# One more attention layout for batches 1 to 7: shared query rows, wider transposes, one transpose burst

## The chip, the cores and the metric

The kernel runs on one core of one Trainium2 chip. The metric is the device time of one execution in microseconds (us); lower is better. The engines are named as in the profile: PE (TensorE matmul), PEld (its weight loads), DVE (VectorE), ACT (ScalarE), POOL (GpSimd) and SP (SyncE, which here only issues DMAs).

## What is computed

Eight batches of attention with eight heads, 576 positions and 64 columns per head, are followed by a MoE layer without routing. The attention has two parts that are added. One is local: each position attends to the positions less than 4 away. The other is coarse: q, k and v are averaged over groups of 4 positions, 144 rows attend to 144 rows, and each result row is repeated 4 times. Cut to its core:

```python
out_d = sm_attn(mean4(q), mean4(k), mean4(v))      # 144 x 144 per head
out_up = np.repeat(out_d, 4, axis=2)
scores = np.where(abs(i - j) < 4, scale * q @ k.T, -1e9)
out_local = softmax(scores) @ v
x = (out_up + out_local).transpose(0, 2, 1, 3).reshape(B * S, H * D)   # 4608 x 512
h = x @ w_in                                       # 512 x 2048
return (h / (1 + exp(-1.702 * h))) @ w_out         # 2048 x 512
```

## The kernel before

**Groups and steps.** The MoE runs over nine groups of 512 tokens. A group has 64 matmuls of 512 columns for the first layer (`mm1`, line 717 in `hps_mm`) and 64 for the second (`mm2`, line 781). While group g runs, the attention of batch g + 1 is put between these matmuls in steps written out by hand: `attention` (line 666) returns a list of functions, and `POS` (line 810) says ahead of which step of the group each is issued. Steps below 16 count blocks of four matmuls of `mm1`; from 16 on, step n stands ahead of matmul n - 16 of `mm2`. Group 0 has its own list, `POS_0` (line 811). Batch 0 is computed ahead of all groups by functions of its own (names ending in 0).

Every engine executes its instructions in program order. What a step issues on ACT or DVE therefore stands ahead of what later matmuls need from these engines.

**One batch.** Two head pairs share a score step. `scores_mixed` (line 401) writes local and coarse scores into three double banks of PSUM (`PA`, three tiles of two banks each), ACT exponentiates them (lines 415 and 421), and DVE multiplies the local ones by the mask (line 429). Then four head pairs `hp` follow, each through these stages:

- `av` (line 431): 20 local and 20 coarse matmuls of 65 columns (64 of v and one that gives the sum for the normalisation), in 64x64 tiles of the array. The local rows come in five chunks with two key halves (`par`), for two heads `j`. Rows of head 0 and head 1 lie on different halves of the partitions (`pos = j if par == 0 else 1 - j`).
- `normalise` (line 476): a reciprocal and a multiplication on DVE, from PSUM into y in bf16.
- `transp` (line 491): 20 matmuls with the identity for the local part and 6 for the coarse part, in 64x64 tiles, into an fp32 double bank x.
- `copy_od` (line 620): ACT copies the coarse part out of x, each column four times, into od in fp32; od has two buffers.
- `merge` (line 637): DVE adds x and od into `xT`, which `mm1` of the next group reads. One addition takes 570 columns and a second one the 6 columns at both ends.

In batches 2 to 7 the steps are: scores 0, exponentials 0, scores and exponentials 1, `av` and `normalise` of pairs 0 and 1 (step 45), `av` of pairs 2 and 3 with `transp` of pair 0 (step 56), `transp` and `merge` of pairs 1 to 3 (step 69). Batch 1 has nine steps: `av` of pairs 0 and 1 (46), `transp` of 0 (52), of 1 (56), `av` of 2 and 3 (65), `transp` of 2 (71), of 3 (75).

**Output and loads.** When 16 matmuls of `mm2` have filled a bank, ACT evicts it into osb (line 766) and SP stores it. Two single banks (`PM`) take turns there; `mm1` uses the same two, and for its second tile one bank of PA. In group 0, `mm2` holds four output tiles at once, two of them in PA[0]. The loads of q and k are issued by POOL, those of v by SP; `load_v4` follows the last step of the batch.

Of the kernel before, what the change touches and what calls it, by code (L numbers as in the profile page):

```python
# [8 lines left out]
FP32 = mybir.dt.float32  # L9
BF16 = mybir.dt.bfloat16  # L10
AF = mybir.ActivationFunctionType
ALU = mybir.AluOpType
# [7 lines left out]
def kernel(  # L20
# [409 lines left out]

    def av(b, hp, n=None):
        o = ps_tile(n)
        av_local(b, hp, o)
        av_down(b, hp, o)
        return o

    def banks(t):
        return t if t is PM else [t[:, u, :] for u in range(2)]

    def av_local(b, hp, o, chunks=range(5)):  # L440
        E, vb, o = es[hp], vbs[b % 2], banks(o)
        for i in chunks:
            for par in range(2):
                for j in range(2):
                    pos = j if par == 0 else 1 - j
                    nc.tensor.matmul(  # L446
                        o[par][64 * pos : 64 * pos + 64, 65 * i : 65 * i + 65],
                        lhsT=E[64 * par : 64 * par + 64, j, 60 * i : 60 * i + 64],
                        rhs=vb[64 * par : 64 * par + 64, i, 2 * hp + j, :],
                        start=True, stop=True,  # L450
                        tile_position=(64 * par, 64 * pos),
                    )

    def av_down(b, hp, o):
        Ed, vd, u, o = eds[hp // 2], vds[b % 2], hp % 2, banks(o)

        blocks = [(kc, x, 0) for kc in range(3) for x in range(2)]
        blocks += [(0, 0, 1), (0, 1, 1), (1, 0, 1), (2, 0, 1)]
        if True:
            for kc, x, c2 in blocks:  # L460
                for j in range(2):
                    pos = j if x == 0 else 1 - j
                    c0 = 65 * (5 + c2)
                    q0 = SD * kc + 48 * (min(x + c2, 1) + x)
                    last = x == c2 == 1
                    if last:
                        q0 = 0
                    nc.tensor.matmul(  # L468
                        o[j][64 * pos : 64 * pos + 64, c0 : c0 + 65],
                        lhsT=Ed[64 * j : 64 * j + 48, u, q0 : q0 + 64],  # L470
                        rhs=vd[64 * j : 64 * j + 48, kc, hp, :],
                        start=(kc == 0), stop=(kc == 2 or last),
                        tile_position=(64 * j, 64 * pos),
                    )

    def normalise(o):
        y = work.tile([128, 2, 7, D], BF16, name="y", tag="y", bufs=4)
        rc = work.tile([128, 2, 7, 1], FP32, name="rc", tag="rc")
        for xs in (slice(0, 1), slice(1, 2)) if o is PM else (slice(0, 2),):
            n = xs.stop - xs.start  # L480
            ov = (o[xs.start][:, None, :] if o is PM else o)[:, :, 0:455].rearrange(
                "p x (c e) -> p x c e", e=65
            )
            nc.vector.reciprocal(rc[:, xs], ov[:, :, :, 64:65])
            nc.vector.tensor_tensor(  # L485
                out=y[:, xs], in0=ov[:, :, :, 0:D],
                in1=rc[:, xs].to_broadcast([128, n, 7, D]), op=ALU.mult,
            )
        return y

    def transp(y, n=None):
        x = ps_tile(n)
        for i in range(5):
            for par in range(2):
                for j in range(2):
                    pos = j if par == 0 else 1 - j
                    c0 = 0 if (par == 1 or i == 0) else 3
                    c1 = 60 if (par == 0 or i == 4) else 57
                    nc.tensor.matmul(  # L499
                        x[64 * j : 64 * j + 64, par, 57 * i + c0 : 57 * i + c1],  # L500
                        lhsT=y[64 * pos : 64 * pos + 60, par, i, :],
                        rhs=ident(pos, 60, c0, c1),
                        start=True, stop=True,
                        tile_position=(64 * pos, 64 * j),
                    )
        for c2, xx in ((0, 0), (0, 1), (1, 0)):
            for j in range(2):
                pos = j if xx == 0 else 1 - j
                nc.tensor.matmul(  # L509
                    x[64 * j : 64 * j + 64, xx, 288 + 48 * c2 : 336 + 48 * c2],  # L510
                    lhsT=y[64 * pos : 64 * pos + 48, j, 5 + c2, :],
                    rhs=ident(pos, 48, 0, 48),
                    start=True, stop=True,
                    tile_position=(64 * pos, 64 * j),
                )
        return x

    def av_local0(hp, o, chunks):
        E, vb = es[hp], vbs[0]
# [98 lines left out]
            )  # L618

    def copy_od(x):  # L620
        od = work.tile([128, S], FP32, name="od", tag="od")
        for xx, t0, n in ((0, 0, 96), (1, 96, 48)):
            nc.scalar.copy(  # L623
                out=od[:, 4 * t0 : 4 * (t0 + n)].rearrange("p (t f) -> p t f", f=4),
                in_=x[:, xx, 288 : 288 + n, None].to_broadcast([128, n, 4]),
            )
        return od

# [5 lines left out]

    def merge(b, hp, x, od, eng=None):
        t0 = b * S
        eng = eng or nc.vector
        if eng is nc.gpsimd:  # L640
            xs = work.tile([128, 2, 512], BF16, name="xs", tag="xs", bufs=2)
            nc.scalar.copy(out=xs[:, :, 0:288], in_=x[:, :, 0:288])
            x = xs
        eng.tensor_tensor(  # L644
            out=sub(xT[hp], t0 + 3, (57, 2), (114, 5), (1, 57)),
            in0=sub(x, 3, (509, 2), (57, 5), (1, 57)),
            in1=sub(od, 3, (57, 2), (114, 5), (1, 57)),
            op=ALU.add,
        )
        eng.tensor_tensor(  # L650
            out=sub(xT[hp], t0, (573, 2), (1, 3)),
            in0=sub(x, 0, (512 + 285, 2), (1, 3)),
            in1=sub(od, 0, (573, 2), (1, 3)),
            op=ALU.add,
        )

    def warm(n, cols=512, t=None, z=wz):
        t = pm_tile() if t is None else t  # L660
# [5 lines left out]
    def attention(b, slots=None):  # L666
# [23 lines left out]
                    st["y", hp] = normalise(st["o", hp])  # L690
            return f

        def tr(*hps):
            def f():
                for hp in hps:
                    st["x", hp] = transp(st["y", hp], slots and slots[hp % 2])
                for hp in hps:
                    od = copy_od(st["x", hp])
                    merge(b, hp, st["x", hp], od)
            return f  # L700
# [5 lines left out]
        def av_tr():  # L706
            for hp in (2, 3):
                st["o", hp] = av(b, hp)
            st["x", 0] = transp(st["y", 0])
            for hp in (2, 3):  # L710
                st["y", hp] = normalise(st["o", hp])
            merge(b, 0, st["x", 0], copy_od(st["x", 0]))

        return first + [av_tr, tr(1, 2, 3)]

    def hps_mm(g, ffc, dmc, acc):
        nc.tensor.matmul(  # L717
# [261 lines left out]
```

## Time and profile before

| what | value |
|---|---|
| median of 3 runs | 320.72 us (318.91 to 321.6) |
| profiled execution, own time | 320.13 us |
| its span, first to last instruction | 318.4 us |
| mean granted TensorE clock | 0.995 |
| instructions | 10941 |
| DMA packets | 64078, 40.02 MB |

The span is what the profile shows; the execution's own time is 1.7 us longer, for what lies around it. A line of the profile names the source line, the engine, the operation, what is written and read (out<-in), the count, the busy time or the mean duration, and the idle time before it with what ended it. "issue" as the releaser means that the engine waited for nothing that the profile shows. Durations of matmuls include their latency, so that many overlap; starts say more than durations. Some matmul records are missing from the trace; the weight loads are all there.

### The profile page before, as it was taken

How to read it: one execution, taken by the hardware profiler on the slowest of the kernel's cores; microseconds unless marked ns; L12 is line 12 of the kernel's file. 1: busy time of each engine (PE TensorE's matmuls, PEld its weight loads, DVE VectorE, ACT ScalarE, POOL GpSimd, SP SyncE). 2: the span in 40 equal slices, each digit the busy share in tenths (PEclk: the TensorE clock that was granted, in tenths of full speed). 3: DMA queues.
4: the chain of work that ended last, by engine and by line, in shares of the span. 5: the costliest groups of instructions: out<-in, count | busy, mean ns of one | idle time of the engine just before them, and what ended most of it. 6: DMA issues, size and time to landing. Idle time of an engine off the chain costs nothing.

```text
span 318.4 us, 10941 instructions
## 1 busy us (share of the span) xinstructions
PE 301.9 (95%) x4872; PEld 156.5 (49%) x4923; DVE 130.3 (41%) x219; ACT 184.9 (58%) x320; POOL 138.7 (44%) x170
## 2 busy tenths in 40 slices
PE   7699999999899999999999999999999999999995
PEld 4465454545454555445545454445445544444444
DVE  5855625831575047704780288017811650000000
ACT  5445782567546684659465846584667556415611
POOL 8773790099227940695059604980294000000000
PEclk9979999999999999999999999999999999999999
DMA  7999999999949923995299619961810210020011
GB/s 120 118 200 209 182 126 213 166 229 227 165 128 203 207 64 103 190 209 101 72 197 205 128 48 213 206 136 39 176 41 3 70 68 2 0 99 33 2 65 67
DMA packets 64078, 40.02 MB, mean 126 GB/s; under 512 B 44064, under 2 KB 55456, under 8 KB 64032
## 3 DMA queue, kind: packets, MB, share of 16 engines
q1 hardware_dynamic: 44496, 24.32, 37.3%
q0 software_dynamic: 19392, 14.95, 33.8%
q8 instruction: 38, 0.62, 0.9%
q14 instruction: 8, 0.07, 0.1%
q10 hardware_dynamic: 144, 0.07, 0.1%
HBM read 44.83 MB, written 9.44 MB: 170 GB/s over the span
## 4 chain that ended last, share of the span: by engine, by line
PE 91%; issue 3%; DMA 2%; DVE 1%; POOL 1%; ACT 1%; POOLq 0%
PE pm L781 35%; PE pm L717 35%; PE pa L717 4%; PE pa L365 2%; PE pa L377 2%; DMA qb<-in_q_dram 2%; PE pa L781 2%; PE pa L446 2%; PE pa L499 2%; PE pa L468 2%; PE pm L796 1%; PE pm L334 1%; PE pa L509 0%; PE pa L524 0%; DVE qT L267 0%
## 5 line engine op out<-in xcount | busy, mean ns | idle before, releaser
L717 PE MATMUL pm<-xT,w_in_bf 128*128 128x512 bf16 x495 | 118.2, 379 | 1.2 <-ACT xT L616 0.2
L781 PE MATMUL pm<-w_out_bf,gT 128*128 128x512 bf16 x499 | 114.4, 379 | 4.2 <-issue 4.1
L728 ACT ACTIVATE gT<-pm 128x512 bf16<-128x512 f32 x128 | 76.3, 598 | 43.7 <-PE pm L717 43.7
L717 PEld LDWEIGHTS <-w_in_bf 128*128 128x128 bf16 x576 | 55.7, 98 | 66.5 <-issue 0.5
L781 PEld LDWEIGHTS <-gT 128*128 128x128 bf16 x560 | 52.1, 98 | 60.1 <-issue 0.8
L429 DVE TENSOR_TENSOR es<-es,mask 128x600 bf16<-128x600 bf16 x28 | 17.6, 643 | 94.6 <-ACT es L415 93.8
L297 POOL TENSOR_TENSOR pq<-kT 128x576 f32<-128x576 bf16 x13 | 15.1, 1165 | 70.5 <-DVE kT L267 70.5
L766 ACT ACTIVATE osb<-pm 128x512 f32<-128x512 f32 (+2 forms) x35 | 20.5, 586 | 38.2 <-PE pm L781 30.3
L623 ACT COPY od<-pa 128x384 f32<-128x384 f32 (+1 forms) x56 | 19.0, 407 | 27.2 <-PE pa L509 20.7
L485 DVE TENSOR_TENSOR y<-pa,rc 128x896 bf16<-128x896 f32 x28 | 30.6, 1092 | 1.0
L415 ACT ACTIVATE es<-pa 128x600 bf16<-128x600 f32 x32 | 19.7, 668 | 9.5 <-PE pa L365 9.4
L644 DVE TENSOR_TENSOR xT<-pa,od 128x570 bf16<-128x570 f32 x28 | 21.0, 752 | 8.8 <-ACT od L623 8.8
L313 POOL TENSOR_TENSOR v<-v 112x512 f32<-112x512 f32 x18 | 23.0, 1279 | 0.0
L768 DVE TENSOR_SCALAR osb<-pm 128x128 f32<-128x128 f32 x1 | 0.3, 291 | 55.0 <-ACT osb L766 55.0
L267 DVE STREAM_TRANSPOSE kT<-kb 128x576 f32<-128x576 f32 x16 | 20.0, 1250 | 4.3 <-DMA kb<-in_k_dram 4.2
L267 DVE STREAM_TRANSPOSE qT<-qb 128x576 f32<-128x576 f32 x16 | 19.9, 1242 | 0.6 <-POOL kdT L301 0.2
L717 PE MATMUL pa<-xT,w_in_bf 128*128 128x512 bf16 x64 | 20.0, 379 | 0.0
L307 POOL CAST vb<-vf 128x2560 bf16<-128x2560 f32 x6 | 13.9, 2319 | 13.7 <-DMA vf<-in_v_dram 11.3
L365 PEld LDWEIGHTS <-kT 32*64 32x64 bf16 x1280 | 14.2, 104 | 7.7 <-issue 4.9
L365 PE MATMUL pa<-qT,kT 32*64 32x60 bf16 x1280 | 16.4, 198 | 1.3 <-DVE qT L267 1.3
L221 POOL DMA_DIRECT2D vb<-in_v_dram x20 | 13.7, 698 | 9.1 <-DMA w_in_bf<-in_moe_w_in_dram 4.0
L297 POOL TENSOR_TENSOR pq<-qT 128x576 f32<-128x576 bf16 x14 | 16.0, 1145 | 0.1
(90 smaller groups left out, 274.2 us busy)
## 6 DMA issues: line engine op xcount, KB each, us to landing
out_dram<-osb SPq DMA_DIRECT2D x35, 256.0 KB, 2.1
vf<-in_v_dram SPq DMA_DIRECT2D x60, 128.0 KB, 6.8
v<-in_v_dram SPq DMA_DIRECT2D x36, 192.0 KB, 5.5
kb<-in_k_dram POOLq DMA_DIRECT2D x16, 288.0 KB, 7.2
qb<-in_q_dram POOLq DMA_DIRECT2D x16, 288.0 KB, 8.6
w_in_bf<-in_moe_w_in_dram POOLq DMA_DIRECT2D x4, 512.0 KB, 7.2
w_out_bf<-in_moe_w_out_dram POOLq DMA_DIRECT2D x4, 512.0 KB, 12.9
vb<-in_v_dram POOLq DMA_DIRECT2D x20, 64.0 KB, 6.4
```

Of the source, the lines that this page charges most:

```text
L267: nc.vector.transpose(out=t32.rearrange("p (i c) -> p c i", c=18), in_=store[b, qd].bitcast(FP32).rearrange("p (c d) -> p c d", c=18),)
L297: nc.gpsimd.tensor_tensor(out=t1, in0=sv[:, :, 0:2, :], in1=sv[:, :, 2:4, :], op=ALU.add)
L313: eng.tensor_tensor(out=t1[0:112], in0=x[:, :, 0:2, :], in1=x[:, :, 2:4, :], op=ALU.add)
L365: nc.tensor.matmul(sp[r // 2][64 * par : 64 * par + 64, r % 2, 60 * i : 60 * i + 60], lhsT=kT[b, qd][rows, k0 : k0 + 64, a], rhs=qT[b, qd] ...
L415: nc.scalar.activation(out=es[2 * qd + u][:, :, 0:300], in_=sp[u][:, :, 0:300], func=AF.Exp, scale=inv_sqrt_d,)
L485: nc.vector.tensor_tensor(out=y[:, xs], in0=ov[:, :, :, 0:D], in1=rc[:, xs].to_broadcast([128, n, 7, D]), op=ALU.mult,)
L623: nc.scalar.copy(out=od[:, 4 * t0 : 4 * (t0 + n)].rearrange("p (t f) -> p t f", f=4), in_=x[:, xx, 288 : 288 + n, None].to_broadcast([128, ...
L644: eng.tensor_tensor(out=sub(xT[hp], t0 + 3, (57, 2), (114, 5), (1, 57)), in0=sub(x, 3, (509, 2), (57, 5), (1, 57)), in1=sub(od, 3, (57, 2) ...
L717: nc.tensor.matmul(acc, lhsT=w_in_bf[:, dmc, ffc * 128 : (ffc + 1) * 128], rhs=xT[dmc][:, g * TG : g * TG + TG], start=(dmc == 0), stop=(d ...
L728: nc.scalar.activation(out=gT[:, ffc, :], in_=acc, func=AF.Silu, scale=GELU_SCALE)
L766: eng.activation(out=osb, in_=ap, func=AF.Copy, scale=1.0 / GELU_SCALE)
L781: nc.tensor.matmul(ops[t], lhsT=gT[:, ffc, t * 128 : (t + 1) * 128], rhs=w_out_bf[:, ffc, :], start=(ffc == 0), stop=(ffc == n_ffc - 1),)
```

## The change

For batches 1 to 7:

- `av` puts both heads of a pair on the same partitions (the chunk decides: `pos = i % 2`), and next to each other in the free dimension; the coarse rows are laid out in pieces of 64, 64 and 16 rows. It has the same 40 matmuls in another order.
- `normalise` writes y as 14 slots, and one copy on ACT moves the slot 12 of the upper half to slot 5.
- `transp` has 13 matmuls in transpose mode. Each takes two slots (both heads, 128 columns) of one half of the partitions in a 64x128 tile, and writes bf16. Half `pos` writes bank `pos`.
- Two pairs share one double bank of x (`x_pair`): pairs 0 and 2, and pairs 1 and 3.
- od is bf16, and its two copies take 64 and 80 rows instead of 96 and 48. `merge` has three additions of 456, 117 and 3 columns.
- The steps are the same six for all seven batches: both `av` steps, and then one step with the transposes of all four pairs and all four merges. The positions are 45, 54 and 65 (in group 0: 46, 54 and 65, and the second score step moves from 30 to 29).

```diff
     def av(b, hp, n=None):
         o = ps_tile(n)
-        av_local(b, hp, o)
-        av_down(b, hp, o)
+        E, Ed, vb, vd, u = es[hp], eds[hp // 2], vbs[b % 2], vds[b % 2], hp % 2
+
+        def local(i, par, j):
+            pos, c0 = i % 2, 65 * (i // 2 * 2 + j + par)
+            nc.tensor.matmul(
+                o[64 * pos : 64 * pos + 64, par, c0 : c0 + 65],
...
+                tile_position=(64 * par, 64 * pos),
+            )
+        def down(kc, j, pos, slot, q0, last=2):
+            nc.tensor.matmul(
+                o[64 * pos : 64 * pos + 64, j, 65 * slot : 65 * slot + 65],
...
+                tile_position=(64 * j, 64 * pos),
+            )
+        for i in (0, 2):
+            for j in range(2):
+                for par, e in ((0, 0), (1, 1), (1, 0), (0, 1)):
+                    local(i + e, par, j)
+        left = [(local, (4, par, j)) for j in range(2) for par in range(2)]
+        left += [(down, (kc, j, 0, 6 - 6 * j, 0)) for kc in range(3) for j in range(2)]
+        right = [(down, (0, j, 1, 5 + j, 64, 0)) for j in (1, 0)]
+        right += [(down, (kc, j, 1, 6 - 6 * j, 64)) for kc in range(3) for j in (1, 0)]
+        right += [(down, (kc, j, 1, 4 + j, 128)) for kc in range(3) for j in (1, 0)]
+        for n in range(len(right)):
+            for side in (left, right):
+                if n < len(side):
+                    side[n][0](*side[n][1])
         return o
...
+        nc.scalar.copy(out=y[64:128, 5, :], in_=y[64:128, 12, :])
+        return y
+
+    def x_pair(n=None):
+        t = ps_tile(n).rearrange("p x n -> p (x n)").bitcast(BF16)
+        t = t.rearrange("p (x n) -> p x n", x=2)
+        return [t[:, :, 512 * u : 512 * u + 512] for u in range(2)]
+
+    def transp(y, x):
+        def put(pos, c0, n, src):
+            nc.tensor.matmul(
+                x[:, pos, c0 : c0 + n], lhsT=src, rhs=ident(pos, src.shape[0], 0, n),
+                is_transpose=True, start=True, stop=True, tile_position=(64 * pos, 0),
+            )
+
+        for m in range(3):
             for par in range(2):
+                for pos in range(2 if m < 2 else 1):
+                    c0 = 8 * par + 2 * m
+                    put(pos, 120 * m + 60 * par, 60, y[64 * pos : 64 * pos + 60, c0 : c0 + 2, :])
+                if m == 2:
+                    c0 = 6 - 2 * par
+                    put(1, 240 + 64 * par, 64, y[64:128, c0 : c0 + 2, :])
+        put(0, 360, 64, y[0:64, 6:8, :])
...
-        od = work.tile([128, S], FP32, name="od", tag="od")
-        for xx, t0, n in ((0, 0, 96), (1, 96, 48)):
+        od = work.tile([128, S], BF16, name="od", tag="od")
+        for xx, c0, t0, n in ((0, 360, 0, 64), (1, 240, 64, 80)):
...
+        for at, col, dims, from_x in (
+            (3, 3, ((228, 2), (114, 2), (1, 114)), ((120, 2), (row, 2), (1, 114))),
+            (459, 243, ((1, 117),), ((1, 117),)),
+            (0, 0, ((1, 3),), ((1, 3),)),
+        ):
...
-        first = [lambda: s_pe(0), lambda: s_act(0), s1, avn(0, 1)]
-        if b == 1:
-            return first + [tr(0), tr(1), avn(2, 3), tr(2), tr(3)]
...
-        return first + [av_tr, tr(1, 2, 3)]
+        def tr():
+            for u in range(2):
+                st["x", u], st["x", u + 2] = x_pair(slots and slots[u])
+            for hp in range(HP):
+                transp(st["y", hp], st["x", hp])
+            for hp in range(HP):
+                merge(b, hp, st["x", hp], copy_od(st["x", hp]))
+
+        return [lambda: s_pe(0), lambda: s_act(0), s1, avn(0, 1), avn(2, 3), tr]
...
-    POS = [13, 16, 35, 45, 56, 69]
-    POS_0 = [16, 18, 30, 46, 52, 56, 65, 71, 75]
+    POS = [13, 16, 35, 45, 54, 65]
+    POS_0 = [16, 18, 29, 46, 54, 65]
```

More of the change, by code (lines that the diff above doesn't have):

```diff
@@ L454, in av_down @@
[L454 to L516, printed above, removed]
+        E, Ed, vb, vd, u = es[hp], eds[hp // 2], vbs[b % 2], vds[b % 2], hp % 2
@@ L633, in sub, with merge @@
         )
-    def merge(b, hp, x, od, eng=None):
+    def merge(b, hp, x, od):
         t0 = b * S
[L639 to L655, printed above, removed]
+        row = x.ap[1][0]
+        for at, col, dims, from_x in (
[3 more added lines that the diff above has]
+        ):
+            nc.vector.tensor_tensor(
+                out=sub(xT[hp], t0 + at, *dims), in0=sub(x, col, *from_x),
+                in1=sub(od, at, *dims), op=ALU.add,
+            )
     def warm(n, cols=512, t=None, z=wz):
```

46 lines of the change are left out of this document (16 added, 30 removed).

## The prediction

> **What bounds the kernel now.** I read the page first: the busy table, then the chain that ended last.
>
> ```profile
> PE 301.9 (95%) x4872; PEld 156.5 (49%) x4923; DVE 130.3 (41%) x219; ACT 184.9 (58%) x320; POOL 138.7 (44%) x170
> PE 91%; issue 3%; DMA 2%; DVE 1%; POOL 1%; ACT 1%; POOLq 0%
> ```
>
> PE is busy for 95% of the span and 91% of the chain, so a microsecond counts only if it is PE's or if PE waits for it. The next view is the table by windows, with windows from one start of a 512-column matmul to another. The columns are length, then PE, PEld, DVE, ACT, POOL with counts, then the granted clock.
>
> ```profile
> 129.83:162.59 32.76, 32.02 (x596) 16.54 (x600) 16.17 (x26) 21.02 (x37) 17.47 (x19) 1.00 0.77 146
> 149.98:151.33 1.35, 1.20 (x82) 0.89 (x82) 1.32 (x4) 1.33 (x2) 0.45 (x1) 1.00 0.00 0
> 153.28:154.85 1.57, 1.41 (x108) 1.12 (x108) 1.00 (x3) 0.01 (x1) 0.00 (x0) 1.00 0.46 167
> 157.23:158.53 1.30, 1.15 (x80) 0.85 (x80) 0.48 (x2) 0.49 (x2) 0.00 (x0) 1.00 0.39 143
> 53.07:53.93 0.86, 0.71 (x28) 0.41 (x28) 0.68 (x1) 0.24 (x2) 0.00 (x0) 1.00 1.11 209
> 50.35:60.91 10.56, 9.57 (x214) 4.96 (x217) 7.68 (x14) 3.90 (x10) 0.18 (x1) 1.00 1.06 195
> ```
>
> The first row is one steady group (a "group" is 512 tokens of the MoE, and carries the attention of the next batch). Weight loads are recorded completely, matmuls not, so I count PEld. The pace of the large matmuls comes from this row of the timeline:
>
> ```profile
> 118.51 2.32 PE L781 MATMUL pm<-w_out_bf,gT 128*128 128x512 bf16 x10 [0.16 <-issue]
> ```
>
> (2.32 - 0.38 for the last one) / 9 = 0.2156 us. 128 of the 600 loads are large: 27.6 us of 32.76. The other 5.2 us are five bursts of small matmuls: two of scores, and three that the change touches. Subtracting 0.2156 us for each large load in a window leaves the price of its burst: 80 AV matmuls 1.35 - 2 x 0.2156 = 0.92; 80 AV and 26 transposes 1.57 - 0.43 = 1.14; 78 transposes 1.30 - 0.43 = 0.87; 26 transposes alone 0.86 - 0.43 = 0.43. From 26 to 78: 0.44 / 52 = 8.5 ns per transpose, and 0.43 - 26 x 8.5 ns = 0.21 us for entering and leaving a burst. The row 50.35:60.91 is batch 1 after its first AV burst: 217 loads are 80 AV, 104 transposes and 33 large, so bursts take 10.56 - 7.11 = 3.45 us.
>
> **The change, part by part.** *AV*: 40 matmuls per pair before and after, in the same 64x64 tiles with the same 11 groups of four: nothing on PE. *Transposes*: 26 per pair become 13, 104 per batch become 52. This is no halving. Before, four 64x64 tiles run side by side, so four transposes share one slot of 4 x 8.5 = 34 ns. A 64x128 tile leaves room for two. The nearest rows are the 48x128 tiles of batch 0 (their form is two row tiles in two banks, as in the change):
>
> ```profile
> 20.66 0.27 PE L547 MATMUL pa<-vd,ed 48*128 48x65 bf16 x6
> 21.86 0.27 PE L547 MATMUL pa<-vd,ed 48*128 48x65 bf16 x6
> L547 PE MATMUL pa<-vd,ed 48*128 48x65 bf16 x24 | 1.1, 194 | 0.0
> ```
>
> Three pairs start within 0.27 - 0.19 = 0.08 us: 38 ns per pair of 65 columns, against 36 ns for a group of four AV matmuls of 65 columns ((0.92 - 0.21) / 20). I take 35 ns for 60 to 64 columns. A pair of heads needs 7 slots (13 is odd and the next begins on the same row half), a batch 28: 0.98 us, where 104 x 8.5 ns were 0.88. The bounds: 52 at the old 8.5 ns each is 0.44 us; two slots' time for every slot, if the halves do not run side by side or the new mode is slower, is 1.96. Transpose mode itself is in no row before; I take 0.98 because L547 has the same tiles, banks and widths.
>
> Batches 2 to 7 keep three bursts: 0.22 (transposes inside AV) + 0.87 = 1.09 becomes 0.98 + 0.21 = 1.19: +0.10 x 6 = **+0.6 us**. Batch 1 had four transpose bursts, 3.45 - 0.92 = 2.53 us with its waits, and gets one of 1.19: **-1.3 us**.
>
> *Scores of batch 1 one matmul earlier (29 for 30)*: the large matmul that takes over their bank waits 0.26 us for the exponentials, of which one matmul's 0.22 goes: **-0.2 us**.
>
> ```profile
> 45.17 1.02 PE L781 MATMUL pa<-w_out_bf,gT 128*128 128x512 bf16 x4 [0.26 <-ACT es L415]
> 126.02 0.75 DVE L644 TENSOR_TENSOR xT<-pa,od 128x570 bf16<-128x570 f32 x1 [1.09 <-ACT od L623]
> 126.88 0.75 DVE L644 TENSOR_TENSOR xT<-pa,od 128x570 bf16<-128x570 f32 x1
> 123.81 0.60 ACT L766 ACTIVATE osb<-pm 128x512 f32<-128x512 f32 x1 [1.07 <-PE pm L781]
> 125.28 1.31 ACT L623 COPY od<-pa 128x384 f32<-128x384 f32 x4 [0.88 <-PE pa L509]
> 82.02 1.03 DVE L429 TENSOR_TENSOR es<-es,mask 128x600 bf16<-128x600 bf16 x2 [1.31 <-ACT es L415]
> 117.46 0.35 PE L446 MATMUL pa<-vb,es 64*64 64x65 bf16 x20
> 119.14 0.60 ACT L766 ACTIVATE osb<-pm 128x512 f32<-128x512 f32 x1 [0.48 <-PE pm L781]
> 119.59 1.09 DVE L485 TENSOR_TENSOR y<-pa,rc 128x896 bf16<-128x896 f32 x1
> L173 ACT ACTIVATE dp<-di,db 128x64 f32<-128x64 f32 x7 | 1.8, 335 | 2.9 <-POOL db L101 2.9
> ```
>
> *Merges and the shared bank.* A merge starts every 0.86 us (126.02 to 126.88), two od copies take 1.31 / 2 = 0.66. The merge becomes three adds (456, 117 and 3 columns for 570 and 6): the same 576 elements and one more start of 0.15. With every operand bf16 it could also run as the mask does, 600 columns in 0.52 us. Between 0.6 and 1.0 us I take 0.9, since every add from PSUM in the trace needs about 1 ns per column. Pairs 0 and 2 share one double bank, so in the built order od 0 waits for the last transpose of pair 2, od 1 for that of pair 3. Counting from the burst's start S: od 0 at S + 1.0, merges start at 1.7, 2.6, 3.5, 4.4, the last ends near 5.3. The next group's first matmul is at S + 1.0 + 15 x 0.2156 = S + 4.3 and needs pair 3 six matmuls later, S + 5.6. Cover 0.3 us: nothing; at 1.0 each, some 0.1 us per batch.
>
> *The same chain in batch 1.* There the evictions of the first two output tiles stand on ACT behind all eight od copies, and od 3 waits for merge 1 (two od buffers). od 3 ends near S + 4.2, the eviction (0.60) near 4.8, and the first matmul of group 1 wants that bank at S + 4.3. Bounds 0 and 0.5; I take **+0.3 us**.
>
> *New copies of y on ACT* (28 of 64x64, about 0.3 us by L173): they wait for DVE's normalise, which ends 3.2 us after the AV burst's start (119.59 + 1.09 against 117.46). The output eviction queued behind them moves from 119.14 to about 121.0; its bank is wanted 16 large matmuls (3.4 us) and a burst later. Pair 3's copy ends 3.5 us after its AV burst starts; its transposes come after 0.92 + 11 x 0.2156 + 0.75 = 4.0. Nothing, on these covers. *Queues*: the v4 loads move up four matmuls with the last step, past no store of SP; POOL's order stays.
>
> *Waits inside bursts.* PE stops in mid-burst with "issue" as the releaser:
>
> ```profile
> 84.51 0.32 PE L468 MATMUL pa<-vd,ed 48*64 48x65 bf16 x16 [0.88 <-issue]
> 88.51 0.21 PE L446 MATMUL pa<-vb,es 64*64 64x65 bf16 x1 [0.19 <-issue]
> 220.57 0.28 PE L499 MATMUL pa<-id,y 60*64 60x57 bf16 x11 [0.17 <-issue]
> 82.95:85.37 2.42, 1.39 (x82) 0.97 (x82) 0.54 (x3) 1.67 (x2) 0.00 (x0) 1.00 1.21 186
> 87.32:89.26 1.94, 1.59 (x108) 1.19 (x108) 1.19 (x3) 0.06 (x1) 1.86 (x1) 1.00 0.36 135
> 215.50:217.17 1.67, 1.39 (x82) 0.97 (x82) 0.90 (x3) 1.49 (x2) 0.00 (x0) 1.00 0.02 7
> 219.12:221.06 1.94, 1.61 (x108) 1.21 (x108) 0.96 (x2) 0.06 (x1) 0.00 (x0) 1.00 0.37 135
> 84.50:88.50 4.00, 3.65 (x127) 2.17 (x128) 2.81 (x5) 0.73 (x2) 1.10 (x1) 1.00 0.63 175
> 216.56:220.56 4.00, 3.67 (x127) 2.18 (x128) 2.86 (x6) 1.04 (x2) 0.00 (x0) 1.00 0.19 70
> q8 instruction: 38, 0.62, 0.9%
> ```
>
> Against 0.92 and 1.14, these four bursts lose 1.07, 0.37, 0.32 and 0.37: 2.1 us. From one wait's end to the next lie exactly 128 loads, 256 instructions, and 4.00 us, twice. The program has 38 instruction packets for some 9850 PE instructions, 256 each. So I read them as waits for the next block of instructions, which come where 256 instructions pass too fast. In the program's order all these waits sit at the same place of a block. Placing the same edges in the changed order, with the prices above, before has eight blocks that would take 3.4 to 3.7 us (mean 3.54); 2.1 / 8 = 0.27 us each, so a block needs about 3.8. The changed order, whose two AV bursts stand 9 instead of 11 matmuls apart, has four of 3.4 and three of 3.2 (119 small, 9 large): 4 x 0.4 + 3 x 0.6 = 3.4 us. **+1.3 us**; bounds -2.1 (none waits) and +2.8 (all need 4.0). The Trainium skill, Runtime: NRT & Kernel Launch, Instruction fetch mechanics, has the blocks of 256 but calls the cost of a boundary mostly hidden; by it the term is nil and the sum 319.5. The four bursts speak against it.
>
> **Sum.** -1.3 + 0.6 - 0.2 + 0.3 + 1.3 = +0.7 us on the profiled execution's own 320.13 us: 320.8. That execution lies 0.6 us under the median shown, 320.72, so the forecast is no change that can be told.
>
> **Rivals.**
> *Transposes cost twice a slot* (slower). The mechanism: row halves in turn, or a mode at half pace. Price 0.98 x 7 = 6.9: 327.7 us. It decides once a slot costs over 50 ns (0.015 x 28 x 7 = 2.9). For it: no such instruction is in the trace. Against: L547 shows halves side by side, and the clock is 1.00 in every window. The Trainium skill, TensorE: Matmul & The Clock Gate, Part 4, says that the full clock does not engage for transposes in this mode; that speaks against the change, and no row here can show it yet.
> *Transposes at the old price per instruction* (faster): -0.54 x 7 = -3.8, 317.0 us. For it: 52 fewer per batch. Against: at 8.5 ns a pair would take 17 ns for 60 columns, half of every slot seen.
> *No block waits* (faster): -3.4, 317.4 us. For it: some short blocks passed unharmed before (eight short, four waits). Against: the new ones are shorter.
> *The merges come late in every group* (slower): od 1 waits for the whole burst; if copies or adds on bf16 cost 0.25 more each, pair 3 comes 0.5 us late, x 7: 324.3 us. Against: widths and element counts are the old ones.
>
> **How the numbers follow.** Chances: the forecast 0.50 (319 to 322.5 by the bounds of its small terms), double slots 0.17, old price 0.12, no block waits 0.13, late merges 0.08. About 1% is what a measurement of this kernel can tell from no change: 317.5 and 323.9. Faster 0.12 + 0.13 = 0.25, slower 0.17 + 0.08 = 0.25, same 0.50. The range 317.0 to 325.0 takes in all but double slots: 0.17 left out.
>
> **What would show it.** The windows of the transpose burst: a price of 1.2 us for 52 puts is right; 0.65 or 2.2 are the rivals. Batch 1 should lose about 1.3 us between its first AV burst and group 1. Gaps with "issue" inside AV bursts, 256 instructions apart, show the blocks; a gap before the first `mm1` matmul of a group, released by DVE or ACT, shows the merges or the eviction. I am wrong if the transpose slot is far from 35 ns.

## The result, and the profile after

The changed kernel takes 317.85 us, the median of 15 runs (316.99 to 319.58); the kernel before took 320.44 in 15 runs beside them (318.8 to 323.11). The ratio is 0.993, with a 95% interval of 0.9908 to 0.9952. A later set of 12 against 24 runs gave 0.9952 (0.9923 to 0.998). So the change gains 1.5 to 2.6 us, 0.5 to 0.7%. The forecast was 320.8, no change.

The page after, its busy table and its chain, with the DMA queue that carries instructions:

```profile
PE 299.6 (95%) x4509; PEld 155.1 (49%) x4559; DVE 124.6 (40%) x247; ACT 190.4 (60%) x348; POOL 138.9 (44%) x170
PE 89%; DMA 4%; issue 3%; POOL 1%; DVE 1%; ACT 1%; POOLq 0%
q8 instruction: 35, 0.57, 0.8%
```

PE still bounds the kernel. It has 364 weight loads fewer (7 x 52) and 35 instruction packets for 38. The table by windows follows, with the columns of the prediction's: a steady group; an AV burst of 80; a transpose burst of 52, in a steady group and in batch 1; three AV bursts with pauses; and all of group 0.

```profile
124.56:157.25 32.69, 31.95 (x544) 16.45 (x548) 15.38 (x31) 22.04 (x42) 17.47 (x19) 1.00 0.78 148
147.98:149.34 1.36, 1.21 (x82) 0.91 (x82) 1.36 (x3) 1.34 (x2) 0.69 (x1) 1.00 0.00 0
154.18:155.60 1.42, 1.27 (x54) 0.96 (x54) 0.31 (x1) 1.05 (x3) 0.00 (x0) 1.00 0.16 59
54.04:55.47 1.43, 1.27 (x54) 0.95 (x54) 0.00 (x0) 0.56 (x3) 0.00 (x0) 1.00 1.13 229
80.55:83.55 3.00, 1.41 (x82) 0.99 (x82) 1.46 (x3) 1.73 (x3) 0.00 (x0) 1.00 0.72 138
114.87:116.42 1.55, 1.40 (x82) 0.98 (x82) 1.55 (x1) 1.49 (x2) 1.55 (x1) 1.00 0.01 5
117.93:119.54 1.61, 1.41 (x82) 0.99 (x82) 1.57 (x4) 0.27 (x2) 0.00 (x0) 1.00 0.00 0
22.78:58.28 35.50, 34.29 (x583) 18.13 (x586) 18.35 (x33) 22.71 (x44) 17.62 (x23) 1.00 1.40 184
```

A steady group went from 32.76 to 32.69: 0.07 shorter, where 0.10 more was forecast. A transpose burst costs 1.43 - 2 x 0.2156 = 1.00, where 1.19 was forecast; less the 0.21 of entering and leaving, 0.79 / 28 = 28 ns a slot instead of 35. The clock stays at 1.00 in it. The same row of group 0 before, and that of group 1:

```profile
23.75:60.70 36.95, 34.93 (x634) 18.32 (x639) 19.47 (x28) 22.62 (x40) 16.86 (x22) 1.00 1.36 181
60.70:94.90 34.20, 32.39 (x596) 16.68 (x601) 16.05 (x24) 21.50 (x37) 20.07 (x20) 1.00 0.92 185
```

In this pair of profiles the groups changed by -1.45 (group 0), +0.14 (1), +0.27 (2), -0.07 each (3, 4, 6) and -0.76 (5); groups 7 and 8 carry no attention and kept their length. That is -2.0 us. The other 1.0 of the span (318.4 to 315.4) lies ahead of group 0, in code that the change leaves alone: group 0 began at 23.75 before and 22.78 after, but at 24.48 and 24.31 in a second profile of each and at 23.38 in a third one after. It scatters within one kernel by more than the two differ, so it is not counted as the change's.

### The profile page after: what moved, and what is told of

Read it like the earlier page. It is cut to its first block, busy times and chain, and to the rows that moved or that the text cites. A ratio compares the mean times of both kernels' runs of the same rounds, so it can differ in the third digit from the quotient of the medians.

```text
span 315.4 us, 10252 instructions
## 1 busy us (share of the span) xinstructions
PE 299.6 (95%) x4509; PEld 155.1 (49%) x4559; DVE 124.6 (40%) x247; ACT 190.4 (60%) x348; POOL 138.9 (44%) x170
## 2 busy tenths in 40 slices
DMA packets 64076, 39.97 MB, mean 127 GB/s; under 512 B 44065, under 2 KB 55457, under 8 KB 64033
## 4 chain that ended last, share of the span: by engine, by line
PE 89%; DMA 4%; issue 3%; POOL 1%; DVE 1%; ACT 1%; POOLq 0%
PE pm L744 35%; PE pm L680 35%; PE pa L680 4%; PE pa L365 2%; DMA qb<-in_q_dram 2%; PE pa L744 2%; PE pa L437 2%; PE pa L488 2%; PE pa L377 2%; PE pa L446 2%; DMA vb<-in_v_dram 1%; PE pm L759 1%; POOL vb L221 0%; POOL kb L190 0%; DVE y L474 0%
## 5 line engine op out<-in xcount | busy, mean ns | idle before, releaser
L429 DVE TENSOR_TENSOR es<-es,mask 128x600 bf16<-128x600 bf16 x28 | 20.2, 732 | 97.8 <-ACT es L415 96.9
L478 ACT COPY y<-y 64x64 bf16<-64x64 bf16 x28 | 6.7, 241 | 29.9 <-DVE y L474 29.9
L630 DVE TENSOR_TENSOR xT<-pa,od 128x456 bf16<-128x456 bf16 (+2 forms) x84 | 16.6, 254 | 13.0 <-ACT od L608 12.9
L608 ACT COPY od<-pa 128x256 bf16<-128x256 bf16 (+1 forms) x56 | 18.3, 408 | 1.6 <-PE pa L488 0.9
```

The source lines that it names most:

```text
L429: nc.vector.tensor_tensor(out=ev, in0=ev, in1=mask, op=ALU.mult)
L608: nc.scalar.copy(out=od[:, 4 * t0 : 4 * (t0 + n)].rearrange("p (t f) -> p t f", f=4), in_=x[:, xx, c0 : c0 + n, None].to_broadcast([128, n ...
L630: nc.vector.tensor_tensor(out=sub(xT[hp], t0 + at, *dims), in0=sub(x, col, *from_x), in1=sub(od, at, *dims), op=ALU.add,)
```

## The experiments

Fourteen variants were profiled, and the two kernels three times more, each time beside the kernel before (319.0 to 320.7 us). "Group" is the number of the MoE group; the batch is one higher. Where expectations speak of pauses in group 6, group 5 is meant, which carries batch 6.

### Both kernels again, and the price of a transpose

*after_again* and *before_again* are the two kernels unaltered.

> The changed kernel unaltered, profiled a second time. If the waits inside AV bursts belong to the order of the instructions (blocks of 256), they come again at the same instructions, 1.6 us in group 1 above all, and the span stays within 0.3 us of 315.4. If they are chance meetings with transfers, they come at other places or with other lengths. The 0.97 us by which group 0 started earlier than in the profile of before is chance if it goes away here or comes in the second profile of before as well.

> The kernel before unaltered, profiled a second time. By the block theory the four waits of 1.07, 0.37, 0.32 and 0.37 us come again at the same instructions; by the rival, chance, they move. Group 0 started at 23.75 us in the first profile; a start near 22.8 here would show that the 0.97 us belong to the run and not to the change.

*twice*: all transposes of a batch are issued twice. *plain*: the first time without transpose mode, into the same banks as fp32.

```diff
+            for hp in range(HP):
+                transp(st["y", hp], st["x", hp])
             for hp in range(HP):
                 transp(st["y", hp], st["x", hp])
```

> Each batch from 1 to 7 does its 52 transposes twice, the second time over the first (same results). This prices 28 more slots with nothing for entering or leaving. By the profile of after (a burst of 1.00 us less 0.21 for its ends, 28 ns a slot) a batch costs 0.79 us more, seven 5.5 us: 323.3 us beside 317.8. By the 35 ns of the prediction it is 0.98 and 6.9 us: 324.7. If a burst has a fixed part of its own that does not repeat (a change of mode, say 0.3 us), the second 52 cost only 0.5 a batch, 3.5 us in all.

> Ahead of the 52 transposes of each batch stand the same 52 products as ordinary matmuls with the identity (no transpose mode), in the same 64x128 tiles, written in fp32 to the same double banks and then overwritten by the real ones (same results). If the mode makes the slot cheap, the ordinary ones cost the 35 ns of the 48x128 tiles of batch 0: 0.98 us more a batch, 6.9 us in all. If the tile and its 60 to 64 columns do it, they cost the same 28 ns: 0.79 a batch, 5.5 us in all. Cadence of the pairs in the trace: 35 or 27 to 28 ns.

*narrow*, *t64_60*, *t64_30*, *one_half* and *t32_60* put other matmuls in the place of the first set, one line each:

```diff
# narrow: 64x128 tiles, 30 columns         # t64_60, t64_30: 64x64 tiles
+  put(pos, 120*m + 60*par, 30, ...)       +  lhsT=y[64*pos : 64*pos+60, n, :], rhs=ident(pos, 60, 0, 60)
# one_half: 64x128, one half of the rows   # t32_60: 64x32 tiles
+  lhsT=y[0:60, n : n+2, :]                +  lhsT=y[64*pos : 64*pos+60, n, 0:32]
```

> Ahead of the 52 transposes of each batch stand 52 ordinary matmuls in the same 64x128 tiles that read only 30 to 32 columns of the identity (results overwritten). The slot of two cost 28 ns with 60 to 64 columns. If the columns set the slot (60 at 2.4 a ns are 25 ns), half of them cost 15 to 17 ns, 0.4 to 0.5 us more a batch. If something per slot or per instruction sets it, 28 ns and 0.78 us a batch.

> Ahead of the 52 transposes of each batch stand 104 ordinary matmuls in 64x64 tiles, four to a slot, 60 columns each (results overwritten): the kind of before, in the place of after. By the price of before (8.5 ns each, 34 ns a slot) 0.88 us more a batch, where the same data in 52 of 64x128 cost 0.78. If the old price was too high because of the old place (bursts of 26), 26 slots of 28 ns: 0.73.

> The same 104 matmuls in 64x64 tiles with 30 columns each. If each matmul and its weight load take 8.5 ns whatever they do, a slot of four stays at 34 ns and a batch pays the same 0.88 us as with 60 columns. If the columns set the slot, it falls to 15 to 17 ns and 0.4 to 0.45 us a batch.

> Ahead of the 52 transposes of each batch stand 52 ordinary matmuls in 64x128 tiles that are all on the same half of the rows, 60 columns (results overwritten). On both halves in turn 52 cost 0.78 us, 15 ns each. If two run side by side in a slot of 28 ns, as the prediction counted, these have no partner: 28 ns each, 1.46 us more a batch. If each matmul with its weight load has a price of its own, whatever its neighbour, 15 ns and 0.78 us.

> The same place, 104 matmuls in 64x32 tiles (32 columns of weights instead of 64, 60 columns each; results overwritten). In 64x64 tiles 104 cost 1.00 us, 9.6 ns each, with 60 and with 30 columns alike, and 64x128 tiles 15 ns each. If the width of the weight load sets the price of one, it falls below 9.6, to 6 to 7 ns, 0.6 to 0.75 us a batch. If there is a floor per matmul and weight load, 9 to 9.6 ns and 0.95 to 1.0 us stay.

The windows of the burst, in the order twice, plain, narrow, t64_60, t64_30, one_half, t32_60:

```profile
159.10:161.10 2.00, 2.00 (x107) 1.64 (x105) 0.29 (x1) 0.88 (x3) 0.00 (x0) 1.00 0.03 8
```
```profile
157.76:159.76 2.00, 2.00 (x106) 1.64 (x104) 0.30 (x1) 0.87 (x3) 0.00 (x0) 1.00 0.04 8
```
```profile
158.67:160.80 2.13, 1.97 (x106) 1.66 (x106) 0.29 (x1) 1.10 (x3) 0.00 (x0) 1.00 0.06 17
```
```profile
125.04:127.46 2.42, 2.27 (x158) 1.92 (x158) 0.29 (x1) 1.09 (x3) 0.00 (x0) 1.00 0.18 62
```
```profile
127.08:129.49 2.41, 2.26 (x158) 1.92 (x158) 0.29 (x1) 1.10 (x3) 0.00 (x0) 1.00 0.18 62
```
```profile
161.13:163.77 2.64, 2.64 (x107) 2.28 (x105) 0.29 (x1) 0.88 (x3) 0.00 (x0) 1.00 0.24 84
```
```profile
123.24:125.39 2.15, 2.15 (x159) 1.73 (x157) 0.29 (x1) 0.88 (x3) 0.00 (x0) 1.00 0.07 24
```

Each window runs from the start of one large matmul to the start of the next large one that follows the burst, or of the one after that. Where it has 106 or 158 loads, two of them are of large matmuls; in twice, one_half and t32_60 (105, 157) one is. In plain the load of the first large matmul lies just outside the window (104), and one is taken off. Less 0.2156 us for each of these, and less the 1.00 of the real transposes:

| set put first | us more | per matmul | per slot of two halves |
|---|---|---|---|
| twice: 52 in transpose mode | 0.78 | 15.0 ns | 28 ns |
| plain: 52 ordinary | 0.78 | 15.0 ns | 28 ns |
| narrow: 52 of 30 columns | 0.70 | 13.5 ns | 25 ns |
| one_half: 52 on one half | 1.42 | 27.4 ns | 27.4 ns for one |
| t64_60: 104 in 64x64 | 0.99, with 0.09 for the change of tiles | 8.7 ns | 32 ns for up to four |
| t64_30: the same, 30 columns | 0.98, with 0.08 | 8.7 ns | 32 ns for up to four |
| t32_60: 104 in 64x32 | 0.93, with 0.10 | 8.0 ns | not counted |

In the last three rows PE changes from 64x64 or 64x32 tiles to the 64x128 of the transposes in mid-burst. In t64_60:

```profile
125.34 1.07 PE L507 MATMUL pa<-id,y 60*64 60x60 bf16 x104
126.35 0.43 PE L488 MATMUL pa<-id,y 60*128 60x60 bf16 x18
```

Less some 0.19 us for the last one, the 104 starts span 0.88 us, and the first transpose starts 0.12 us after the last of them (0.11 in t64_30, 0.13 in t32_60), where slots follow each other in 0.03. The difference is the price of the change, and the columns per matmul and per slot are without it.

Four things follow. Transpose mode costs nothing of its own (twice and plain agree). Two halves do run side by side: without a partner a matmul takes 27.4 ns, with one the two take 28. In 64x128 tiles the columns matter little: 30 of them take 25 ns a slot and 60 take 28; what sets the 25 is not shown. In 64x64 tiles the price is 8.7 ns (8.5 in the prediction) for each matmul with its load, with 30 columns as with 60, and with half the weight columns (64x32) it is still 8.0. Whether each matmul or each slot sets it stays open: in t64_60 and t64_30 the starts come in groups 31.7 ns apart, and the 104 make 28 groups, because here, too, 13 is odd; in t32_60 most come singly, 8.3 ns apart. The Trainium skill, TensorE: Matmul & The Clock Gate, Part 2, Back-to-back issue gap, gives N / 2.4 + 2.5 ns for N columns without the weight loads, and a floor of about 25 ns up to 64 columns. For 60 columns the first is an estimate of 27.5 ns, which one_half agrees with (27.4); narrow agrees with the floor (25).

*twice* was timed at 324.95 us, 1.0141 (1.0065 to 1.0217) of before. That is nearer to the 324.7 of a 35 ns slot than to the 323.3 of 28 ns. The time is no measure of the slot here: the profiled execution has a pause of 1.8 us inside the transposes of group 0, and a group without pauses is 0.79 longer than the 32.69 of the changed kernel:

```profile
197.97:231.45 33.48, 33.48 (x601) 17.24 (x600) 14.54 (x30) 21.89 (x40) 17.48 (x19) 1.00 0.76 144
```

The others were timed in one execution each: plain 324.87 us, narrow 324.5, one_half 330.34, t32_60 327.43, t64_60 330.86 and t64_30 332.99.

### Batch 1, the positions, od

*b1_four* gives batch 1 its four bursts back, with the new tiles. *pos_old* puts back the old positions of batches 2 to 7, *od_fp32* the old type of od.

```diff
-        return [lambda: s_pe(0), lambda: s_act(0), s1, avn(0, 1), avn(2, 3), tr]
+        if b == 1:
+            return first + [one(0), one(1), avn(2, 3), one(2), one(3)]
...
-    POS = [13, 16, 35, 45, 54, 65]
+    POS = [13, 16, 35, 45, 56, 69]
...
-        od = work.tile([128, S], BF16, name="od", tag="od")
+        od = work.tile([128, S], FP32, name="od", tag="od")
```

> The changed kernel, but batch 1 keeps the nine steps of before: its transposes and merges stand one pair at a time at the old positions, in four bursts, with the new tiles. By the prediction's first term (four bursts for one) it is 1.3 us slower than the changed kernel, about 319.1, all of it in group 0. The rival, that the gain of group 0 comes from the cheaper slots or from chance: 317.9 to 318.2, group 0 at its 35.5 us.

> The changed kernel with the old positions for batches 2 to 7 (second AV step at 56 for 54, transposes at 69 for 65). The prediction gave the positions nothing but the place of the block edges. Theory: the bursts cost the same, and groups without waits stay at 32.69 us; a difference comes only where a block of 256 PE instructions now passes in more time, at most 1 us. Rival: the last merges come late for the next group, since the transposes stand four matmuls later (0.86 us): the first mm1 matmuls of groups 2 to 7 would wait, up to 0.8 us each, 4 us in all: 321.8.

> The changed kernel with od in FP32 as before; everything else is as changed. The merges of after run 456 columns in 0.40 us, twice the pace that was assumed (0.9 us for a merge of three adds). If bf16 operands are the reason, the same adds take about 0.6 us for 456 columns here and a merge 0.9 us, and the end of the chain moves back by about 1 us: the eviction in batch 1 then costs 0 to 0.5 us and the steady groups 0 to 0.1 each, 317.9 to 319. Rival: PSUM as a source sets the pace, and the adds stay at 0.40 us; nothing changes.

b1_four took 318.6 us (ratio to before 0.995, 0.9912 to 0.9987), and its group 0 is 35.88 us, 0.38 longer than after's. Two of its bursts:

```profile
50.89:51.50 0.61, 0.61 (x15) 0.25 (x14) 0.58 (x3) 0.24 (x1) 0.18 (x1) 1.00 1.07 200
58.02:58.63 0.61, 0.61 (x16) 0.26 (x14) 0.03 (x1) 0.53 (x2) 0.00 (x0) 1.00 0.56 121
```

A burst of 13 costs 0.61 - 0.2156 = 0.39; four are 1.58, one of 52 is 1.00: three entries fewer are worth 0.58. Of this the changed order gives 0.26 back. In after, the second AV burst of batch 1 stops in the middle, between its two pairs, from 51.13 to 51.40: the second pair writes the bank that DVE's normalise of pair 1 is still reading, which ends at 51.34:

```profile
50.25 1.09 DVE L474 TENSOR_TENSOR y<-pa,rc 128x896 bf16<-128x896 f32 x1
50.98 0.35 PE L446 MATMUL pa<-vd,ed 48*64 48x65 bf16 x17
51.40 0.32 PE L437 MATMUL pa<-vb,es 64*64 64x65 bf16 x17
```

In b1_four that burst comes eleven large matmuls later and does not stop. Both theories were wrong: one burst for four is worth neither 1.3 nor nothing.

pos_old took 318.66 (0.9931, 0.9895 to 0.9967), with 32.69 us in groups without pauses: the positions are worth nothing, and the merges have four matmuls to spare.

od_fp32 took 319.56 (0.9951, 0.9919 to 0.9984). The merges in after, and then here (duration of the shortest, median and longest):

```profile
L630 DVE TENSOR_TENSOR xT<-pa,od x84: 148/209/406, 55.9 to 256.6; 128x456 bf16<-128x456 bf16 x28, 128x117 bf16<-128x117 bf16 x28, 128x3 bf16<-128x3 bf16 x28
```
```profile
L630 DVE TENSOR_TENSOR xT<-pa,od x84: 150/269/636, 56.4 to 260.4; 128x456 bf16<-128x456 bf16 x28, 128x117 bf16<-128x117 bf16 x28, 128x3 bf16<-128x3 bf16 x28
59.47 0.38 PE L680 MATMUL pm<-xT,w_in_bf 128*128 128x512 bf16 x1 [0.25 <-ACT osb L729]
```

With od in bf16 the 456 columns take 0.41 us, with FP32 0.64, though the other source is in PSUM both times. And with FP32 the wait that the prediction named appears: ACT's eviction comes late for the first `mm1` matmul of group 1. In after, where the merges are done sooner, no such wait is in the trace:

```profile
55.15 2.72 ACT L608 COPY od<-pa 128x256 bf16<-128x256 bf16 x8 [0.87 <-PE pa L488]
55.88 1.20 DVE L630 TENSOR_TENSOR xT<-pa,od 128x456 bf16<-128x456 bf16 x6 [1.87 <-ACT od L608]
57.76 1.11 ACT L729 ACTIVATE osb<-pm 128x512 f32<-128x512 f32 x2
```

Six adds (two merges) take 1.20 us; 1.8 were counted. ACT copies all eight od in one run of 2.72 us and never waits for a merge. By their times (0.9951 and 0.993 of before) the two kernels cannot be told apart.

### The pauses in the bursts

*shift64* puts 64 one-column matmuls more ahead of group 0, so that every block edge moves by half a block. *no_loads* leaves out the loads of q, k and v for batches 3 to 7, which compute with the data of batch 2 (so its output is another one). *spread* and *wide* move the steps apart; *after_2* is the changed kernel.

```diff
+    warm(64, 1)
...
-                load_v(b + 1)
+                vf[b + 1] = vf[2]
...
-    POS = [13, 16, 35, 45, 54, 65]
+    POS = [13, 16, 33, 45, 58, 68]      # spread
+    POS = [13, 16, 35, 45, 58, 68]      # wide
```

> The changed kernel with 64 more one-column matmuls ahead of group 0, which moves every later edge of a block of 256 PE instructions by half a block. Theory: the pauses at the four old places inside AV bursts are gone, and those that there are stand at the edges of the new count, 128 instructions before the old ones; a block passes free if it takes over about 4 us. Rival: the pauses belong to these bursts for another reason (a semaphore, a buffer, transfers that meet them) and stay at the same instructions. The time alone says little: 317 to 319.5.

> The changed kernel without the loads of q, k and v for batches 3 to 7: these compute with the data of batch 2. All instructions of PE, ACT and DVE are the same and in the same order; the output is that of other inputs. Theory: a block of PE instructions comes by DMA, and what makes it late is that its fetch starts late or takes long beside these loads; then the pauses inside AV bursts of groups 1, 2 and 6 (0.4 to 2.8 us at the worst place in the profiles so far) shrink to 0.3 at most, and the span falls to 313.5 to 315. Rival: the time that 256 instructions take decides alone; the pauses at these places stay, 0.2 to 0.6 us each.

> The changed kernel with the steps of batches 2 to 7 farther apart (second scores at 33 for 35, second AV step at 58 for 54, transposes at 68 for 65), so that a block of 256 PE instructions that holds two bursts takes some 0.9 us longer, 4.1 where it took 3.2 to 3.4. Theory: PE's pauses at block edges inside the AV bursts of groups 1, 2 and 6, together 0.5 to 2.5 us in the profiles so far, shrink to under 0.5; 316 to 317.5 beside 317.9. Rival: the pauses do not hang on the time that a block takes, and stay; or the merges come late for the next group after transposes at 68, 0.2 us a group: 317.9 to 319.

> The changed kernel with the second AV step at 58 for 54 and the transposes at 68 for 65, the scores where they were. The run before with the scores two matmuls earlier paid 0.26 us a group for a wait of the scores; without that, groups without pauses should be at 32.69 us again, and the pauses inside AV bursts at 0.8 us in all, where the changed kernel had 2.3. 0 to 1.5 us faster than the changed kernel. Rival: pauses differ from run to run by more than the positions change them, and the two are equal.

> The changed kernel again, timed beside the others of this call on the same chip: 317.9 us, 0.993 of the kernel before. Its pauses inside AV bursts stand at the same instructions as in the two profiles before, with other lengths.

The worst place is near the end of group 1's first AV burst, some 10.7 blocks of 256 from the first instruction, counted in matmuls and weight loads. The same matmuls, the last six of line 446 in that burst, in after, after_again, after_2, od_fp32, no_loads and wide:

```profile
83.11 0.28 PE L446 MATMUL pa<-vd,ed 48*64 48x65 bf16 x6 [1.43 <-issue]
```
```profile
83.45 0.28 PE L446 MATMUL pa<-vd,ed 48*64 48x65 bf16 x6 [0.20 <-issue]
```
```profile
83.79 0.28 PE L446 MATMUL pa<-vd,ed 48*64 48x65 bf16 x6 [0.39 <-issue]
```
```profile
85.41 0.28 PE L446 MATMUL pa<-vd,ed 48*64 48x65 bf16 x6 [2.56 <-issue]
```
```profile
83.25 0.28 PE L446 MATMUL pa<-vd,ed 48*64 48x65 bf16 x6 [0.42 <-issue]
```
```profile
85.02 0.28 PE L446 MATMUL pa<-vd,ed 48*64 48x65 bf16 x6 [1.45 <-issue]
```

The place is the program's, the length is each execution's: 0.20 to 2.56 us with identical PE instructions up to there. So it is before the change: the worst place of the first profile (0.88 at 84.51) has no pause in *before_again*, whose longest are 0.75 at 89.27 and 0.61 at 119.54. In shift64 the worst place of after has no pause; its own stand at the new edges, half a block on, at 155.09 and 191.35 (0.32 and 0.35). That the pauses stand at the block edges is shown. The times of the instruction packets in the trace add how: in after, the packet started 2.2 us after the preceding edge (80.32 against 78.08), was moved by 81.61, and PE went on at 83.11. At the eight pauses under 1 us in the AV bursts of groups 1 and 2, in three profiles of the changed kernel, it started 1.0 to 1.6 us after the edge and took 0.9 to 1.6; PE went on 1.3 to 1.6 after it had landed. Together that is 3.4 to 4.1 us, where the matmuls of these blocks need 3.2 to 3.5. Of the pauses over 1.4 us at the worst place, those of after and wide had a packet that started 2.2 us after the edge, and the 2.56 of od_fp32 one that started 3.2 us after. Why it starts late at times is not shown.

The prediction's seven short blocks did not all pause. In group 3 a block of 3.20 us passed free in every profile of this order: the edge ahead of it lies at the very start of a burst, and the packet started 1 us before PE executed the edge (147.21 against 148.28) instead of 1 us after. That PE's sequencer had run ahead through the large matmuls is my reading, and was not tested by itself.

no_loads had 0.42 us at the worst place and pauses at other edges (0.3 and 1.0 us), with 21.61 MB moved instead of 39.97: pauses come without the loads of later batches, too. Whether these loads make the long ones cannot be told from one execution. spread had 0.28 at the worst place, with two more large matmuls in the block ahead of it, and wide 1.45 with the block of the changed kernel. Both lie within the 0.20 to 2.56 of that place, so the scatter hides what the positions do. spread took 318.81 (0.9944, 0.9908 to 0.9981) and lost 0.26 us in each steady group, because its scores, two matmuls earlier, wait for the exponentials; wide took 318.48 (0.9942, 0.9917 to 0.9967) beside after_2's 319.09 (0.9952). No version here beats the changed kernel beyond the intervals.

shift64 took 322.23 us (1.0064, 1.0032 to 1.0096), 4 us more than the changed kernel, and that was not expected. Its group 0 took 40.95 us for 35.50. An edge fell there between the large matmuls after the second AV burst:

```profile
59.16 2.13 PE L744 MATMUL pa<-w_out_bf,gT 128*128 128x512 bf16 x5 [2.05 <-issue]
59.16:61.08 1.92, 1.92 (x5) 0.68 (x5) 0.00 (x0) 0.00 (x0) 0.00 (x0) 0.55 0.79 166
61.64:63.24 1.60, 1.44 (x53) 1.43 (x54) 0.00 (x0) 0.32 (x2) 0.00 (x0) 0.65 0.95 191
```

The last column but two is the granted clock: after the pause it is 0.55 and 0.65, and the five matmuls start 0.43 us apart instead of 0.2156. Another pause of 2.05 us ends at 25.11, at an edge at the start of group 0, and the clock is low after it, too (0.53 from 25.10 to 27.00). These two are the largest differences from the traces of the changed kernel.

## Why the prediction was wrong, step by step

The sum was +0.7 us. Two of its terms failed, the price of the transpose slot and the pauses; two smaller ones were off by 0.3 each. By the runs:

| step of the prediction | forecast | measured |
|---|---|---|
| batch 1, four bursts to one | -1.3 | -0.72 (4 x 0.43 to 1.00); its pauses of 0.8 are counted below |
| batches 2 to 7, transposes | +0.6 | -0.4 (6 x -0.07) |
| scores one matmul earlier | -0.2 | -0.2 |
| eviction behind the od copies | +0.3 | 0 |
| pauses inside bursts | +1.3 | -0.7 on average, by pair of profiles -1.6 to +0.2 |
| not foreseen: bank between the AV pairs of batch 1 | 0 | +0.26 |

- **The slot**: mis-sized, 35 ns for 28. That is 7 x 0.19 = 1.3 us, and the sign of the second term. The mechanism (two halves side by side, so 28 slots a batch) held, as one_half shows. I took the price from three pairs of line 547 and from the four-matmul groups of AV, since both gave 35 to 38. But four 64x64 matmuls take as long with 30 columns as with 60 (t64_30), so their price does not tell how long 60 columns take in a 64x128 slot. Line 547 is not explained by any run: by their starts its three pairs stand 38 and 36 ns apart. The first two pairs of a burst in *twice* stand 39 ns apart as well and the later ones 27 to 28, so three pairs are too few to take a pace from. The agreement of these two rows is what misled me.
- **The pauses**: the step failed in its size. The cause was right (blocks of 256, shift64). The rule that every block under 3.8 us pauses by the difference was not: a quarter of a microsecond was taken as a property of the block, while the same block pauses 0.2 us in one execution and 2.6 in another, and others never. Counting both kernels alike, with the 0.8 that I had booked under batch 1, the pauses are 2.9 and 2.8 us in two profiles before and 2.1, 1.3 and 3.0 in three after. The number of instruction packets fell from 38 to 35, and no rise of 1.3 is seen.
- **Batch 1**: -1.3 was near the -1.45 of group 0 by luck. Without pauses the bursts gave -0.72; 0.8 us of what I called the price of four bursts were pauses of that one execution, +0.26 came new, and -0.2 are the scores. In the third profile of the changed kernel a pause of 0.90 at 58.22 took most of it back (group 0: 36.57).
- **The eviction**: the chain was right and od_fp32 shows it at 0.25 us. It needs the adds at the pace of before, as od_fp32 has it (0.64 us for 456 columns; before, 0.75 for 570, which is 1.3 ns a column and not the 1 of the prediction); with bf16 they took 0.41. I had named that possibility and kept to the rows before, all of which had an fp32 source.
- **The scores**: right. The large matmul that waited 0.26 us for the exponentials starts without a wait in all three profiles after.
- **The rivals**: double slots fell to the clock of 1.00 and the 28 ns. The rule of the Trainium skill quoted there, TensorE: Matmul & The Clock Gate, Part 4, does not show here: the clock is 1.00 in every transpose burst of the windows above. These bursts last 1 to 2 us among other matmuls, so longer runs of transposes are not tested. No block waits was nearest in time (317.4), but the pauses were there; the old price per instruction gave 317.0, but a transpose in a 64x128 tile costs 15 ns, not 8.5. Late merges did not come.

The clean terms (-0.72, -0.4, -0.2, +0.26) make -1.1 us, the pauses of these few profiles -0.7 on average; the medians differ by 1.6 to 2.6. How much of the difference of the medians belongs to pauses cannot be settled with three and two profiles.

## What to carry to other kernels

Price small matmuls by tiles of their own shape: here a matmul with its load took 8.0 to 8.7 ns in 64x64 and 64x32 tiles whatever its columns, and a slot of two halves took 25 to 28 ns in 64x128 tiles for 30 to 60 columns. Check with a second set of the same matmuls before trusting a row that merely looks alike, and look at the starts, since a change of tile shape is in the window as well (0.1 us here). Fewer, wider tiles also shorten the instruction stream, and each entry to a burst that is saved was worth 0.2 us (0.58 for three). Book pauses of a single execution separately from the price of the work, since they don't repeat in size.

## What the runs showed of the hardware that was not expected

- A pause of PE at a block edge can cost more than itself: after 2.05 us in shift64 the granted clock was at half for 3.41 us. After 2.56 us in od_fp32 it stayed at 1.00, so the length alone does not decide. The traces show what differs. In every profile the changes of the clock lie whole multiples of 3.41 us apart, and whether half clock comes goes with how long PE was idle in the stretch of this grid before. First two rows of shift64, then two of od_fp32, counted on from its change at 5.69:

```profile
55.94:59.35 3.41, 1.22 (x5) 0.50 (x7) 2.01 (x3) 0.48 (x2) 0.00 (x0) 1.00 1.03 167
59.35:62.76 3.41, 3.41 (x51) 1.70 (x51) 0.00 (x0) 0.00 (x0) 0.00 (x0) 0.50 0.89 180
80.78:84.19 3.41, 2.07 (x80) 1.13 (x78) 2.19 (x4) 2.58 (x4) 0.15 (x1) 1.00 1.24 204
84.20:87.61 3.41, 2.04 (x14) 0.96 (x15) 1.34 (x2) 0.51 (x3) 0.00 (x0) 1.00 0.82 192
```

  The pause of shift64 lies in one stretch, in which PE is busy for 1.22 us; that of od_fp32 (82.85 to 85.41) is split by an edge, and PE is busy for 2.07 and 2.04. The limit is not sharp: over all profiles, between 21 and 290 us, stretches with 2.05 to 2.19 us idle were followed by half clock each time (four), two with 1.80 were not, and one with 1.68 was. The Trainium skill, TensorE: Matmul & The Clock Gate, Part 1, speaks of a free-running window of about 3.4 us; the traces agree with that length.
- A longer stream of small instructions pays more than its own price. t64_30 took 332.99 us and t64_60 330.86, where 7 x 0.99 on top of the changed kernel's 317.85 would be 324.8; the rest are pauses, among them 1.9 and 2.1 us inside the added matmuls of group 0, and the half clock after these (6.8 and 3.4 us of it).
- An add of 456 columns with a bf16 source in PSUM and a bf16 source in SBUF took 0.41 us, and 0.64 where the second source was FP32.
